# Gate and value weight blocks of a fused attention and two expert layers: prepared in two steps during the attention, with another order of the products behind it

## Chip, cores and metric

One core of one Trainium2 chip. The metric is the device time of one launch in microseconds (us). TensorE does the matrix products, VectorE and ScalarE the elementwise work, GpSimd a part of it, SyncE issues all DMA transfers. Most executions of this kernel agree within 0.3%.

## The reference, cut to what matters

```python
attn_out = _attn_ref(q, k, v)             # 2 batches, 8 heads, 576 positions, 64 wide
x = attn_out.transpose(0, 2, 1, 3).reshape(1152, 512)
# first layer: one wide gated layer, 1536 hidden
g = x @ w_gate
x = (g * (1 / (1 + np.exp(-g)))) * (x @ w_val) @ w_out
# second layer: 8 experts of 1024 hidden, weighted by a routing matrix P of x
for e in range(8):
    out += P[:, e:e+1] * (np.maximum(x @ w1[e], 0) @ w2[e])
```

The attention is the sum of a local one (positions closer than 4) and a pooled one (groups of 4 positions averaged). The weights w_gate, w_val and w_out come as 64-bit floats.

## The kernel before

Three parts follow each other: the attention, the first (gated) layer, the experts. Every product of the layers is made from 16-bit operands: a number is scaled by a power of two and split into a high and a low half, and three products (high x high, high x low, low x high) add up in PSUM (`mm3`, line 171; `split`, line 164).

**Attention** (`attention`, line 346). 16 heads, two to a pair, 8 pairs. For each head: scores on TensorE, row minima and sums on VectorE, exponentials on ScalarE, the division on GpSimd, a transpose on TensorE (`turn`), and for each pair the products with v (`combine`, line 432). `combine` ends with the split of the pair's result into `xhl`, the input of the first layer; the VectorE instruction of that split is kept in `x1_done` (line 463). The scores run 4 heads ahead (`AHEAD`). The generator yields once for each of the 4 heads ahead, then three times a head; in line 655 the loop over it counts these yields as n, so that the pair pr is combined at n = 9 + 6 pr. The SyncE queue loads q, k and v of the pairs (lines 297 to 314).

**Gate and value weights.** The hidden dimension of the first layer is cut into 12 blocks of 128 (`KF1`). A block holds the gate and the value weights for all 512 inputs, 1 MB as 64-bit floats. `prep_gv(f)` (line 207) does all of its preparation: the load into one of two `raw` buffers (line 185); the conversion `from_f64` (line 188) into one of two `cv` buffers, one step on ScalarE (Abs at line 200 or Relu at line 197) and four on VectorE (lines 201 or 198, then 202, 203, 204); the row maxima on ScalarE (line 215), which write over `raw`; the maximum over the partitions (`allmax`, line 147), by two small products and a reduction on VectorE for blocks below `NSHORT` = 6 and on GpSimd (line 155) for the others; the power of two (lines 138 to 141); and the split into one of five `wA` buffers (`WB`), on ScalarE (line 168) and VectorE (line 169). Blocks below `NX` = 3 use Abs, the others Relu.

**First layer.** The positions are cut into two chunks: chunk 0 has 512 columns, all of batch 0, and chunk 1 has 640, the rest. `gv_step(c, f)` (line 506) makes the 24 (chunk 0, 512 wide) or 48 (chunk 1, 320 wide) products of block f with chunk c, then the activation on ScalarE and the product with the value on VectorE (line 547). The first three steps of chunk 0 ("early") use tanh in place of silu and the PSUM banks of a pool that the attention leaves free. A `wA` buffer is free again when both chunks have used its block. `prep_wo(i)` (line 223) prepares two blocks of w_out out of the same `raw` and `cv` buffers. `act_split(c)` (line 556) scales and splits the twelve activations of a chunk; its scales need all of w_out's (line 559), and each of its tiles takes a slot that the activation before has left. `w_out(c)` (line 577) multiplies them by w_out, four output columns of 36 products for chunk 0.

**Order.** Before, blocks 0 and 1 are prepared in the attention's loop (`PREP_AT`), at n = 9 and 21, each behind the last `x1_done` (`tc.issue_after` puts an instruction behind the given one on the same engine, and does nothing on other engines). Then `moe1_step(f)` (line 661) prepares block f + 2, runs chunk 0 on block f and chunk 1 on block f - 3 (`LAG`), and prepares w_out blocks at every second step:

```python
        if f + np_ < KF1:
            prep_gv(f + np_, gv_done.get((0, f - 1)))
        if f < KF1:
            gv_step(0, f, f < NX)
        if f >= LAG:
            gv_step(1, f - LAG, False)
```

The final order on each engine is not this one: a planner walks the program, takes of the instructions that are ready by its own estimate of times the one that stands first in the program, and so may bring later work forward into gaps. On the chip each engine then keeps the planned order.

Of the kernel before, what the change touches and what calls it, by code (L numbers as in the profile page):

```python
# [8 lines left out]
F16 = mybir.dt.float16  # L9
BF16 = mybir.dt.bfloat16  # L10
U32 = mybir.dt.uint32
AF = mybir.ActivationFunctionType
# [7 lines left out]
NT, DM = 1152, 512  # L20
# [6 lines left out]
KF1 = F1 // P  # L27
# [9 lines left out]
FAR = 1.0e9  # L37
DW = 2 * SD
DO = NW * P
PREP_AT = (9, 21)  # L40
AHEAD = 4
NX = 3
LAG = 3
WB = 5
W2B = 6
HSC = 2.0 ** -20
# [3 lines left out]
NWARM = 5  # L50
NQ = 3
V4B = 4
NSHORT = 6
QDV = (0, 1, 2)
SPLITS = (2, 4, 2, 0)

# [2 lines left out]
def tile_kernel(ctx, tc, qT, kT, vw, vd4, wgv, wo, wg2, w1, w2, out):  # L59
# [15 lines left out]
    def tmp(n, nm):  # L75
        return wp.tile([P, 16], F32, tag="tmp", bufs=56, name=nm)[:, :n]
# [106 lines left out]
    def load_f64(src, nm):  # L183
        raw = wp.tile([P, 2 * DM, 2], U32, tag="raw", bufs=2, name=f"raw{nm}")
        nc.sync.dma_start(raw.rearrange("p n w -> p (n w)"), src.bitcast(U32))
        return raw

    def from_f64(raw, nm, relu):

        f = mp.tile([P, 2 * DM], F32, tag="cv", bufs=2, name=f"cv{nm}")
        o, lo, hi = f.bitcast(U32), raw[:, :, 0], raw[:, :, 1]
        h = hi.bitcast(F32)
        if relu:
            A.activation(f, h, AF.Relu, scale=-1.0)
            V.scalar_tensor_tensor(f, h, HI_MIN, f, op0=ALU.max, op1=ALU.max)  # L198
        else:
            A.activation(f, h, AF.Abs)  # L200
            V.tensor_scalar(f, f, HI_MIN, None, op0=ALU.max)
        V.tensor_scalar(o, o, 3, 0x3FFFFFF8, op0=ALU.logical_shift_left, op1=ALU.bitwise_and)  # L202
        V.scalar_tensor_tensor(o, hi, 0xC0000000, o, op0=ALU.bitwise_and, op1=ALU.bitwise_or)  # L203
        V.scalar_tensor_tensor(o, lo, 29, o, op0=ALU.logical_shift_right, op1=ALU.bitwise_or)  # L204
        return f

    def prep_gv(f, after=None):

        w = wp.tile([P, 7 * 4 * P], F16, tag="wA", bufs=WB, name=f"gv{f}")
        w = w[:, :4 * DM].rearrange("p (a n) -> p a n", a=2)  # L210
        raw = load_f64(wgv[f], f"g{f}")
        with tc.issue_after(after.ins) if after else nullcontext():
            src = from_f64(raw, f"g{f}", f >= NX)
            mx = tmp(1, f"mxg{f}")
            A.activation(raw.rearrange("p n w -> p (n w)").bitcast(F16)[:, :2 * DM], src, AF.Abs, accum_out=mx)  # L215
            s, gv_inv[f] = pow2(allmax(mx, 1, f"gv{f}", f < NSHORT), 1, f"gv{f}")
            split(w[:, 0], w[:, 1], src, s)
        gv_w[f] = w
# [4 lines left out]
    def prep_wo(i):  # L223

        ws = [m2.tile([P, 2, DM], F16, tag="wo", bufs=KF1, name=f"wo{i}{j}") for j in range(2)]
        src = from_f64(load_f64(wo[i], f"o{i}"), f"o{i}", False).rearrange("p (j n) -> p j n", j=2)
        mx = tmp(2, f"mxo{i}")
        for j in range(2):
            A.activation(ws[j][:, 0], src[:, j], AF.Abs, accum_out=mx[:, j:j + 1])
        s, _ = pow2(mx, 2, f"wo{i}", wo_inv[:, 2 * i:2 * i + 2])  # L230
        for j in range(2):
            split(ws[j][:, 0], ws[j][:, 1], src[:, j], s[:, j:j + 1])
            wo_w[2 * i + j] = ws[j]
# [83 lines left out]
    x1_done = []  # L317
# [186 lines left out]
    gv_done = {}  # L504
# [51 lines left out]
    def act_split(c):  # L556
        nh = CH[c][1]
        sc = cp.tile([P, KF1], F32, name=f"sc{c}")
        V.tensor_tensor(sc, amx[c], wo_inv, op=ALU.mult)
        s, ia[c] = pow2(allmax(sc, KF1, f"a{c}"), 1, f"a{c}")  # L560
        V.tensor_scalar(sc, wo_inv, s, None, op0=ALU.mult)
        for f in range(KF1):
            t = (m2 if c else mp).tile([P, 2, nh], F32, tag=f"act{c}", bufs=KF1 + 1, name=f"ahl{c}_{f}")
            t = t.rearrange("p u n -> p (u n)").bitcast(F16).rearrange("p (a n) -> p a n", a=2)
            ins = split(t[:, 0], t[:, 1], act[c, f], sc[:, f:f + 1])
            ahl[c, f] = t
        return ins
# [85 lines left out]
    load_v(1)  # L653
    first = tmp(1, "first")
    for n, _ in enumerate(attention()):
        if n in PREP_AT:
            prep_gv(PREP_AT.index(n), x1_done[-1])
    np_ = len(PREP_AT)
    G.partition_all_reduce(first, ones[:, :1], channels=P, reduce_op=RED.max)

    def moe1_step(f):
        if f + np_ < KF1:
            prep_gv(f + np_, gv_done.get((0, f - 1)))
        if f < KF1:
            gv_step(0, f, f < NX)
        if f >= LAG:
            gv_step(1, f - LAG, False)
        if f >= NX and f < KF1:
            prep_wo((f - NX) // 2) if (f - NX) % 2 == 0 else None
        if f == KF1 - 1:  # L670
            for i in range((KF1 - NX + 1) // 2, KF1 // 2):
                prep_wo(i)
            act_split(0)

    for f in range(NX):
        moe1_step(f)
    ctxA.close()
    ctxP = ExitStack()
    psr = ctx.enter_context(tc.tile_pool(name="psr", bufs=1, space=PSUM, reuse_waits="tile"))
    psm = ctxP.enter_context(tc.tile_pool(name="psm", bufs=2, space=PSUM, reuse_waits="tile"))  # L680
    m2 = ctxM.enter_context(tc.tile_pool(name="m2", bufs=1, side="right", reuse_waits="tile"))
    for f in range(NX, KF1 + LAG):
        moe1_step(f)
    ins = act_split(1)
    ctxX.close()
    xp = ctx.enter_context(tc.tile_pool(name="xp", bufs=1, reuse_waits="tile"))
# [156 lines left out]
```

## Time and profile before

| | us |
|---|---|
| three runs | 1053.83, 1054.74, 1056.79; median 1054.74 |
| the profiled execution | 1054.22, of which the span is 1052.4 |
| busy in the span | TensorE 1017.5 (97%), VectorE 752.0 (71%), ScalarE 458.0 (44%), GpSimd 91.5 (9%) |

In the rows below PE is TensorE, PEld its loads of weights, DVE VectorE, ACT ScalarE, POOL GpSimd and SP SyncE; L176 is line 176 of the kernel. Times count from the start of the span. A busy time is a sum over the stretch named, and "x" gives the number of instructions. Idle time of an engine that isn't the bottleneck costs nothing by itself, so the stages are read one by one. In rows of a timeline the bracket at the end is the time that the engine sat idle before, and what ended it. In the rows of busy time by stretch the five columns after the length are PE, PEld, DVE, ACT and POOL. PEclk is the granted clock of TensorE as a share of its full 2.4 GHz.

### The profile page before, as it was taken

The page shows a single profiled execution, that of the slowest core. Times are in us where ns is not written, and L with a number is a line of the kernel's source. Part 1 is how long each engine was busy: PE and PEld are TensorE (multiplying, and loading weights), DVE is VectorE, ACT ScalarE, POOL GpSimd, SP SyncE. Part 2 cuts the span into 40 slices and gives each one's busy share as a digit, 9 for nine tenths or more (in the row PEclk, how much of TensorE's full clock was granted, in tenths as well). Part 3 has the DMA queues.
Part 4 walks back from the last instruction along what each step waited for, and adds up shares of the span by engine and source line. Part 5 has one row for each costly group of instructions (what it writes and reads, how often), then busy time and mean ns, then how long its engine had stood idle before and what let it go on. Part 6 is the DMA issues. An engine that isn't in the chain of part 4 may idle for free.

```text
span 1052.4 us, 16461 instructions
## 1 busy us (share of the span) xinstructions
PE 1017.5 (97%) x6549; PEld 651.2 (62%) x6549; DVE 752.0 (71%) x1552; ACT 458.0 (44%) x957; POOL 91.5 (9%) x125
## 2 busy tenths in 40 slices
PE   6989698999999999999999999999999999999998
PEld 5888254556567866665756756666575675666644
DVE  5695668886691999888759749758874974974631
ACT  6988365666460646345215314414521541441200
POOL 6794000000000200000000000000000000000000
PEclk9999898999999999999999999999999999999999
DMA  9623123331020022112112100301211210020011
GB/s 237 152 79 107 53 108 112 129 128 73 1 81 1 2 80 82 41 40 80 41 40 80 42 23 18 121 1 41 80 41 41 78 44 19 22 81 1 1 40 50
DMA packets 22459, 65.54 MB, mean 62 GB/s; under 512 B 12080, under 2 KB 12336, under 8 KB 15984
## 3 DMA queue, kind: packets, MB, share of 16 engines
q1 hardware_dynamic: 22384, 64.51, 18.0%
q8 instruction: 51, 0.84, 0.3%
q14 instruction: 24, 0.20, 0.1%
HBM read 62.14 MB, written 2.36 MB: 61 GB/s over the span
## 4 chain that ended last, share of the span: by engine, by line
PE 83%; DVE 8%; DMA 4%; ACT 3%; issue 2%; SPq 0%; POOL 0%; ACTq 0%
PE y L176 35%; PE p L176 30%; PE gv L176 7%; PE wo L176 7%; DMA rawg<-in_wgv 2%; DVE cvg L203 1%; PE o L449 1%; DVE cvg L204 1%; PE lgps L575 1%; DMA rawo<-in_wo 1%; ACT rawg L215 1%; DVE cvg L198 1%; DVE cvg L202 1%; DVE xhl L169 1%; DMA qz<-in_qT 0%
## 5 line engine op out<-in xcount | busy, mean ns | idle before, releaser
L176 PE MATMUL y<-w,hhl 128*128 128x512 f16 (+1 forms) x1752 | 396.2, 376 | 0.0
L176 PE MATMUL p<-bop,w 128*128 128x320 f16 (+1 forms) x2688 | 354.4, 286 | 0.8 <-DVE u L715 0.5
L176 PEld LDWEIGHTS <-w 128*128 128x128 f16 x2688 | 263.0, 98 | 90.6 <-issue 1.3
L176 PEld LDWEIGHTS <-hhl 128*128 128x128 f16 x1752 | 171.4, 98 | 178.2
L176 PE MATMUL gv<-xhl,gv 128*128 128x320 f16 (+1 forms) x864 | 147.1, 332 | 7.4 <-ACT gv L168 4.0
L743 ACT ACTIVATE hhl<-h 128x640 f16<-128x640 f32 (+1 forms) x128 | 83.2, 676 | 159.7 <-DVE h L715 159.4
L176 PEld LDWEIGHTS <-gv 128*128 128x128 f16 x864 | 84.9, 99 | 67.0 <-issue 10.5
L168 ACT ACTIVATE w<-r,s_w 128x256 f16<-128x256 f32 (+1 forms) x96 | 71.1, 783 | 115.7 <-PE y L176 86.3
L774 DVE SCALAR_TENSOR_TENSOR acc<-y,pe,acc 128x512 f32<-128x512 f32 (+1 forms) x64 | 47.3, 739 | 101.3 <-PE y L176 100.5
L744 DVE SCALAR_TENSOR_TENSOR hhl<-h,hhl 128x640 f16<-128x640 f32 (+1 forms) x128 | 94.3, 753 | 15.5 <-ACT hhl L743 14.4
L715 DVE SCALAR_TENSOR_TENSOR h<-p,u 128x256 f32<-128x256 f32 (+1 forms) x192 | 84.8, 452 | 19.2 <-PE p L176 13.4
L169 DVE SCALAR_TENSOR_TENSOR w<-r,s_w,w 128x256 f16<-128x256 f32 (+1 forms) x96 | 78.1, 832 | 16.8 <-ACT w L168 16.7
L176 PE MATMUL wo<-ahl,wo 128*128 128x320 f16 (+1 forms) x432 | 71.5, 326 | 0.0
L168 ACT ACTIVATE w<-cmb,s_w 128x512 f16<-128x512 f32 x64 | 43.0, 710 | 40.7 <-DVE cmb L262 38.0
L715 DVE SCALAR_TENSOR_TENSOR u<-p,u 128x320 f32<-128x320 f32 (+1 forms) x128 | 57.2, 447 | 4.1 <-PE p L176 3.2
L176 PEld LDWEIGHTS <-wo 128*128 128x128 f16 x432 | 42.3, 99 | 27.0
L155 POOL PARTITION_ALL_REDUCE g_w<-gm_w x16 | 5.9, 370 | 568.6 <-DVE gm_w L151 562.7
L732 ACT ACTIVATE s<-p 128x256 f32<-128x256 f32 (+1 forms) x64 | 25.4, 397 | 56.7 <-PE p L176 56.7
L145 DVE TENSOR_REDUCE mxw<-r 128x1 f32<-128x1024 f32 x32 | 37.5, 1212 | 12.7 <-DMA r<-in_w 12.7
L169 DVE SCALAR_TENSOR_TENSOR w<-cmb,s_w,w 128x512 f16<-128x512 f32 x64 | 46.1, 740 | 0.0
L282 ACT ACTIVATE j<-r 128x1024 f16<-128x1024 f32 x32 | 33.4, 1046 | 25.1 <-DMA r<-in_w 25.0
L715 DVE SCALAR_TENSOR_TENSOR u<-p,s 128x256 f32<-128x256 f32 (+1 forms) x64 | 28.8, 450 | 5.2 <-PE p L176 4.3
(205 smaller groups left out, 933.5 us busy)
## 6 DMA issues: line engine op xcount, KB each, us to landing
r<-in_w SPq DMA_DIRECT2D x32, 1024.0 KB, 4.8
rawg<-in_wgv SPq DMA_DIRECT2D x12, 1024.0 KB, 6.5
rawo<-in_wo SPq DMA_DIRECT2D x6, 1024.0 KB, 4.8
vz<-in_vw SPq DMA_DIRECT2D x16, 160.0 KB, 3.2
k<-in_kT SPq DMA_DIRECT2D x8, 288.0 KB, 6.3
qz<-in_qT SPq DMA_DIRECT2D x16, 144.0 KB, 5.2
v<-in_vd SPq DMA_DIRECT2D x8, 288.0 KB
out<-acc SPq DMA_DIRECT2D x8, 256.0 KB, 2.0
```

The source lines that it names most:

```text
L145: V.tensor_reduce(o, i, axis=axis, op=ALU.max, apply_absolute_value=True)
L168: return (A.activation(hi, src, AF.Copy, scale=s), V.scalar_tensor_tensor(lo, src, s, hi, op0=ALU.mult, op1=ALU.subtract))
L169: V.scalar_tensor_tensor(lo, src, s, hi, op0=ALU.mult, op1=ALU.subtract))
L176: T.matmul(ps, lhsT=wf(i, k), rhs=xf(j, k), start=n == 0, stop=n == 3 * nk - 1)
L198: V.scalar_tensor_tensor(f, h, HI_MIN, f, op0=ALU.max, op1=ALU.max)
L202: V.tensor_scalar(o, o, 3, 0x3FFFFFF8, op0=ALU.logical_shift_left, op1=ALU.bitwise_and)
L282: A.activation(junk, t[:, 2 * j:2 * j + 2].rearrange("p a n -> p (a n)"), AF.Abs, accum_out=mx[:, 2 * i + j:2 * i + j + 1])
L715: V.scalar_tensor_tensor(o, ps, HSC, u, op0=ALU.mult, op1=ALU.add)
L732: A.activation(s1, p1, AF.Copy, scale=HSC)
L743: ra = A.activation(t[:, 0], h, AF.Relu)
L744: rv = V.scalar_tensor_tensor(t[:, 1], h, 0.0, t[:, 0], op0=ALU.max, op1=ALU.subtract)
L774: V.scalar_tensor_tensor(acc[t][:, ds], ps, p[:, t:t + 1], acc[t][:, ds], op0=ALU.mult, op1=ALU.add)
```

## The change

`prep_gv` is cut into `conv_gv(f)` (load, conversion, row maxima) and `prep_gv(f)` (maximum, power of two, split). In the attention's loop block 0 is converted at n = 4, without a gate. At n = 9 + 6 pr, after the pair pr is combined, block pr is split (pr from 0 to 4) and block pr + 1 converted (pr from 0 to 5), both behind that pair's `x1_done`. Blocks 0 to 6 use Abs (`NABS` = 7), and blocks 0 to 4 the short maximum (`NSHORT` = 5). Behind the attention the three early steps of chunk 0 and its step 3 come first. Then, for g from 0 to 11: chunk 1's products with block g, the split of block g + 5, the conversion of block g + 7 or, from g = 5 on, one pair of w_out blocks, and from g = 1 to 8 chunk 0's products with block g + 3. The last two pairs of w_out blocks and the split of chunk 0's activations follow at g = 8.

```diff
-PREP_AT = (9, 21)
+NABS = 7
-LAG = 3
-NSHORT = 6
+NSHORT = 5
...
+    gv_src = {}
+
+    def gate(after):
+        return tc.issue_after(after.ins) if after else nullcontext()
+
+    def conv_gv(f, after=None):
+
+        raw = load_f64(wgv[f], f"g{f}")
+        with gate(after):
+            src = from_f64(raw, f"g{f}", f >= NABS)
+            mx = tmp(1, f"mxg{f}")
+            A.activation(raw.rearrange("p n w -> p (n w)").bitcast(F16)[:, :2 * DM], src, AF.Abs, accum_out=mx)
+        gv_src[f] = src, mx
+
     def prep_gv(f, after=None):
 
         w = wp.tile([P, 7 * 4 * P], F16, tag="wA", bufs=WB, name=f"gv{f}")
         w = w[:, :4 * DM].rearrange("p (a n) -> p a n", a=2)
-        raw = load_f64(wgv[f], f"g{f}")
-        with tc.issue_after(after.ins) if after else nullcontext():
-            src = from_f64(raw, f"g{f}", f >= NX)
-            mx = tmp(1, f"mxg{f}")
-            A.activation(raw.rearrange("p n w -> p (n w)").bitcast(F16)[:, :2 * DM], src, AF.Abs, accum_out=mx)
+        src, mx = gv_src[f]
+        with gate(after):
             s, gv_inv[f] = pow2(allmax(mx, 1, f"gv{f}", f < NSHORT), 1, f"gv{f}")
             split(w[:, 0], w[:, 1], src, s)
         gv_w[f] = w
...
     for n, _ in enumerate(attention()):
-        if n in PREP_AT:
-            prep_gv(PREP_AT.index(n), x1_done[-1])
-    np_ = len(PREP_AT)
+        pr, r = divmod(n - AHEAD - 5, 6)
+        if n == AHEAD:
+            conv_gv(0)
+        if r == 0 and 0 <= pr < NABS - 1:
+            if pr < WB:
+                prep_gv(pr, x1_done[pr])
+            conv_gv(pr + 1, x1_done[pr])
     G.partition_all_reduce(first, ones[:, :1], channels=P, reduce_op=RED.max)
 
-    def moe1_step(f):
...
     for f in range(NX):
-        moe1_step(f)
+        gv_step(0, f, True)
...
-    for f in range(NX, KF1 + LAG):
-        moe1_step(f)
+    gv_step(0, NX, False)
+    for g in range(KF1):
+        gv_step(1, g, False)
+        if g + WB < KF1:
+            prep_gv(g + WB)
+        if g + NABS < KF1:
+            conv_gv(g + NABS)
+        elif g + NX < KF1:
+            prep_wo(g + NABS - KF1)
+        if 0 < g < KF1 - NX:
+            gv_step(0, g + NX, False)
+            if g + NX == KF1 - 1:
+                for i in range(g + NABS - KF1 + 1, KF1 // 2):
+                    prep_wo(i)
+                act_split(0)
     ins = act_split(1)
```

## Rows read from the trace of the kernel before

**Rows 1.** Busy time by stretch: stretch, length, each engine, PEclk, DMA share, GB/s.
```profile
20.00:41.00 21.00, 18.64 (x158) 17.03 (x156) 10.76 (x39) 18.58 (x77) 18.45 (x23) 0.92 0.77 207
41.00:80.00 39.00, 34.48 (x295) 32.27 (x295) 34.82 (x71) 33.04 (x144) 33.33 (x33) 1.00 0.33 92
80.00:96.00 16.00, 16.00 (x154) 14.64 (x153) 9.30 (x35) 15.25 (x54) 10.48 (x12) 1.00 0.40 113
96.00:107.00 11.00, 11.00 (x75) 7.76 (x73) 6.25 (x16) 5.85 (x14) 0.38 (x1) 1.00 0.21 86
107.00:214.20 107.20, 91.30 (x506) 49.86 (x506) 81.09 (x140) 57.15 (x95) 2.38 (x4) 0.94 0.27 99
214.20:266.30 52.10, 52.10 (x349) 34.08 (x349) 38.80 (x78) 34.70 (x65) 1.92 (x3) 1.00 0.28 102
```

**Rows 2.** Timeline of TensorE around the gate and value products: start, length, what.
```profile
105.06 1.03 PE L449 MATMUL o<-at,vz 128*128 128x120 f32 x8
105.92 1.24 PE L176 MATMUL gv<-xhl,gv 128*128 128x512 f16 x5
114.40 0.58 PE L159 MATMUL sm_gv<-ident,mxg 128*1 128x128 f32 x2 [7.23 <-ACT rawg L215]
...
171.47 4.02 PE L176 MATMUL gv<-xhl,gv 128*128 128x512 f16 x9 [4.00 <-ACT gv L168]
...
259.74 6.68 PE L176 MATMUL gv<-xhl,gv 128*128 128x320 f16 x48
266.26 12.90 PE L176 MATMUL wo<-ahl,wo 128*128 128x512 f16 x59
...
288.38 7.93 PE L176 MATMUL wo<-ahl,wo 128*128 128x512 f16 x36
```

**Rows 3.** Instructions on the converted blocks: ns min/median/max, first and last start.
```profile
L202 DVE TENSOR_SCALAR cvg<-cvg x12: 631/686/694, 42.8 to 209.3; 128x1024 uint32<-128x1024 uint32 x12
L203 DVE SCALAR_TENSOR_TENSOR cvg<-rawg,cvg x12: 1207/1218/1671, 44.7 to 211.0; 128x1024 uint32<-128x1024 uint32 x12
L204 DVE SCALAR_TENSOR_TENSOR cvg<-rawg,cvg x12: 1206/1218/2115, 45.9 to 214.1; 128x1024 uint32<-128x1024 uint32 x12
L215 ACT ACTIVATE rawg<-cvg x12: 1039/1056/1077, 49.7 to 215.8; 128x1024 f16<-128x1024 f32 x12
L168 ACT ACTIVATE gv<-cvg,s_gv x12: 1132/1148/1212, 57.9 to 223.5; 128x1024 f16<-128x1024 f32 x12
L169 DVE SCALAR_TENSOR_TENSOR gv<-cvg,s_gv,gv x12: 1264/1284/2508, 59.8 to 225.2; 128x1024 f16<-128x1024 f32 x12
...
L198 DVE SCALAR_TENSOR_TENSOR cvg<-rawg,cvg x9: 1215/1215/1226, 108.1 to 207.5; 128x1024 f32<-128x1024 f32 x9
L200 ACT ACTIVATE cvg<-rawg x3: 1132/1146/1208, 22.9 to 62.3; 128x1024 f32<-128x1024 f32 x3
L201 DVE TENSOR_SCALAR cvg<-cvg x3: 675/677/683, 41.5 to 67.3; 128x1024 f32<-128x1024 f32 x3
```

**Rows 4.** Timeline of VectorE, small steps of block 0's scale.
```profile
55.41 0.27 DVE L160 TENSOR_REDUCE gr_gv<-sm_gv 1x1 f32<-1x128 f32 x1
...
56.34 0.15 DVE L139 TENSOR_SCALAR u_gv<-u_gv 128x1 uint32<-128x1 uint32 x1
```

**Rows 5.** DMA issues of the page: transfer, count, KB each, median us to landing.
```profile
rawg<-in_wgv SPq DMA_DIRECT2D x12, 1024.0 KB, 6.5
```

**Rows 6.** Who waited for whom, 0 to 100 us: total us, times, longest.
```profile
ACT k L357 <- DMA k<-in_kT: 5.2, 5, 1.4
```

**Rows 7.** Timeline of VectorE from the last evaluation of chunk 0.
```profile
240.49 0.75 DVE L547 SCALAR_TENSOR_TENSOR act<-gv,iv,act 128x512 f32<-128x512 f32 x1
...
247.20 0.88 DVE L547 SCALAR_TENSOR_TENSOR act<-gv,iv,act 128x640 f32<-128x640 f32 x1
...
267.71 0.75 DVE L169 SCALAR_TENSOR_TENSOR ahl<-act,sc,ahl 128x512 f16<-128x512 f32 x1
```

**Rows 8.** GpSimd's additions of line 374: ns min/median/max, first and last start.
```profile
L374 POOL TENSOR_TENSOR vdz<-vt x16: 445/451/3392, 16.1 to 89.5; 72x128 f32<-72x128 f32 x16
```

More of the change, by code (lines that the diff above doesn't have):

```diff
@@ L655, in tile_kernel @@
     for n, _ in enumerate(attention()):
-        if n in PREP_AT:
-            prep_gv(PREP_AT.index(n), x1_done[-1])
-    np_ = len(PREP_AT)
-    G.partition_all_reduce(first, ones[:, :1], channels=P, reduce_op=RED.max)
-    def moe1_step(f):
[L662 to L673, printed above, removed]
+        pr, r = divmod(n - AHEAD - 5, 6)
[5 more added lines that the diff above has]
+            conv_gv(pr + 1, x1_done[pr])
+    G.partition_all_reduce(first, ones[:, :1], channels=P, reduce_op=RED.max)
     for f in range(NX):
-        moe1_step(f)
+        gv_step(0, f, True)
     ctxA.close()
```

## Prediction

> **What bounds the kernel now.** I read the page first, then the busy time of each engine by stage, then TensorE's instructions in order of time, then the durations of the operations that the change moves. From 214 us to the end of the stage at 266 TensorE is busy all the time [rows 1], and 97% of the whole span; the profiled execution took 1054.22 us for a span of 1052.4, 0.5 below the median of 1054.74. So the change can win only ahead of 214 us. There are two stages there. The **attention** (to 106 us) is crowded: between 41 and 80 us VectorE is busy 34.82 of 39 us, ScalarE 33.04, GpSimd 33.33 and TensorE 34.48; from 80 to 96 us TensorE is full and ScalarE has 0.75 us left [rows 1]. The **gate/value stage** from 107 to 214 us is where TensorE idles: 91.30 busy of 107.20 us, 15.9 us lost, at a mean granted clock of 0.94, so part of it ran at the lower level, 1.2 for 2.4 GHz [rows 1]. The reader is to see there that TensorE runs out of finished weight blocks: 7.23 us for the maximum of block 3, later 4.00 us for a split [rows 2].
>
> How much is there to win? The attention's last product starts at 105.06 us; at 107.16 the first gate block's 24 products for chunk 0 are done, and the first w_out product starts at 266.26 [rows 2]: 159.1 us. A 512-wide product costs (12.90 - 7.93)/(59 - 36) = 0.2161 us, two uninterrupted runs of w_out subtracted so that their tails cancel; a 320-wide one (266.26 - 259.74)/48 = 0.1358 [rows 2]. A chunk-0 step is thus 24 x 0.2161 = 5.19 us and a chunk-1 step 48 x 0.1358 = 6.52. Left to do are 11 x 5.19 + 12 x 6.52 = 135.3 us. **23.8 us is the most that can be won**: 15.9 of idle time, the rest products at the lower clock level, small maximum products and waits inside the order.
>
> **The change, part by part.** *More blocks in the attention.* Before, blocks 0 to 2 are converted and split by 107 us. After, 0 to 6 are to be converted and 0 to 4 split. One conversion costs VectorE 0.677 + 0.686 + 1.218 + 1.218 = 3.80 us and ScalarE 1.146 + 1.056 = 2.2; one split costs VectorE 1.284 and ScalarE 1.148 [rows 3], and its scale four VectorE steps of 0.15 and a reduce of 0.27 [rows 4], so VectorE 2.2 in all. By stage:
> - 20 to 41 us: conversion 0 moves here from 41 to 47 us. VectorE has 10.2 us free, GpSimd only 2.55 [rows 1]. The two-input steps (2.4 us) hold GpSimd up; bounds 0 and 2.4, I take 1.2, since half of its free time is there.
> - 41 to 80 us: three conversions as before, but three splits in place of one: 2 x 2.2 = 4.4 us more for VectorE, which has 4.2 free. An engine whose queue waits on three others won't reach 100%: at its present 89%, 4.4/0.89 = 4.9 us longer. Bounds 0.2 (every gap filled) and 4.9; I take 4.9, because GpSimd is as full as VectorE. ScalarE's 2.3 more fit in its 6 free.
> - 80 to 96 us: conversion 4 comes in, one split stays one: 3.8 for VectorE (6.7 free) and 2.2 for ScalarE (0.75 free): 1.5 us longer, bounds 0 and 2.2.
> - 96 us and later: split 4, conversions 5 and 6, some 9.8 us of VectorE beside 15 us or more of early products that need none of it: nothing. Were that cover gone, it costs up to 9.8.
>
> Together the attention's end moves back by **7.6 us** (bounds 0.2 and 9.5).
> *Gates.* The prepared steps stand behind a pair's last VectorE split, on the same engine: no semaphore, but the score minima of later heads queue behind them; that is in the 4.9.
> *Loads.* The same twelve, in the same SyncE queue, but loads 2 to 6 now go between the pairs' loads. 6.5 us from issue to landing, and ScalarE waits only 5.2 us in five waits for k now [rows 5, 6]. I take nothing; the bound is the last rival.
> *Abs in place of Relu* for blocks 3 to 6: VectorE 1.215 becomes 0.677 [rows 3], 2.2 us in all, already in the sums above. *The maximum of block 5* goes from TensorE to GpSimd, which does nothing then: nothing.
> *The new order of products.* Five ready blocks give 4 x 5.19 + 6.52 = 27 us of products before block 0's buffer must be refilled, and each round brings 11.71 us of products for one conversion, one split and two evaluations, about 8 us of VectorE (4.3 + 2.2, and 0.75 + 0.88 for the evaluations [rows 7]). So late weights (7.23 and 4.00) vanish. What stays is short waits for the evaluation that frees PSUM: 15.9 - 11.2 = 4.7 us before. I take **4** (bounds 0, as from 214 to 266 us with VectorE 74% busy, and 8).
> *The end of the stage.* Before, four chunk-1 steps follow the last chunk-0 step; after, three. The chain behind it is: the last chunk-0 evaluation ends at 241.24, the twelfth activation split at 268.46 [rows 7], while w_out's twelfth block is first used 33 products in, at 266.26 + 33 x 0.2161 = 273.4. 4.9 us of slack less one step of 6.52 makes 1.6 us of waiting. The last two w_out blocks are also prepared later against that step, and the scales need them: bounds 0 and 10 (two blocks' chains). I take **2.5**, near the row.
>
> Sum: 23.8 - 7.6 - 4 - 2.5 = 9.7 us won; 1054.22 - 9.7 = 1044.5 on the profiled execution, **1045 us** against the median. After the first w_out product all is TensorE-bound and moves rigidly.
>
> **A row against the change.** Where VectorE's two-input steps meet GpSimd's, one of the two is stretched: a split took 2.508 us where the median is 1.284, L204 2.115 for 1.218 [rows 3], and a GpSimd add 3.392 for 0.451 [rows 8]. The Trainium skill (SBUF — State Buffer, section "SBUF: two separate sides") calls the shared port pair an exclusive lock, held for a whole instruction, with the other side fully blocked. The rows agree that somebody waits; by the rule the whole added work would come on top of GpSimd's, which is the second rival below.
>
> **Rivals.** *The gaps hold it* (0.16): attention 3 us longer, short waits 2, none at w_out; 18.8 won, 1036. For: 10.2 and 6.7 us free on VectorE on either side of the crowd. Against: the middle has 4.2.
> *VectorE and GpSimd take turns throughout* (0.12): by 92 us two more conversions and two more splits' long steps, 2 x 3.80 + 2 x 1.284 = 10.2 us, lengthen GpSimd's run, plus ScalarE's 1.5: 23.8 - 11.7 - 6.5 = 5.6 won, 1049. For: the stretched rows. Against: GpSimd is idle 5.5 of 16 us from 80 us on [rows 1].
> *The change doesn't do what it says* (0.08): the order on each engine is planned from estimated times, and the gates only set an earliest point; blocks 3 and 4 may be split only after the attention. Then the 11.2 us of waits stay and the attention grows by 3: 23.8 - 11.2 - 4 - 2.5 - 3 = 3.1 won, 1051.6.
> *w_out waits its full 10 us* (0.06): 2.1 won, 1052.6.
> *Slower* (0.15): the queue of SyncE issues in order, so a 1 MB block load can stand in front of a pair's k and q. ScalarE takes k in its own order and stops there, with the exponentials behind it. Four pairs (4 to 7) at 6.5 us [rows 5] are 26 us; 23.8 - 26 - 6.5 = 8.7 lost, 1063. It decides from the point where the attention's last product starts later than 105 + 17 = 122 us. For: k is already waited for. Against: the DMA engines are less than half busy after 41 us [rows 1].
>
> **How the numbers follow.** The forecast itself has 0.43 (1039 to 1050). About 0.3% (3.2 us) is what a measurement here can tell from no change. Faster by more: 0.41 of the forecast, 0.16, 0.12 and 0.03 of the third rival make 0.72. Within: 0.02, 0.05, 0.06 make 0.13. Slower: 0.15. The range from 1034 to 1056 leaves out the slow rival and a corner of the fast one, 0.18.
>
> **What would show it.** Right: block 4's split ends before or within 5 us of the attention's last product, which starts near 113 us; after it TensorE has no idle time above 2 us until w_out, whose first product starts near 256 to 257 us; a short wait inside w_out's first column, ended by the activation split. Wrong: block loads in front of k in SyncE's queue with ScalarE waiting on DMA; attention past 122 us; waits for weight splits above 4 us; or a first w_out pass with gaps of 5 us and more.

## The result, and the profile after

The changed kernel takes 1045.34 us (median of 4 runs, 1044.92 to 1047.23), the kernel before, beside it, 1054.28: a ratio of 0.9915 (0.9893 to 0.9936), 8.9 us faster. The profiled execution took 1045.74 us, its span is 1043.7, 8.7 below that of before.

Busy time by stretch of the kernel after, with the columns of [rows 1]:

```profile
20.00:41.00 21.00, 16.69 (x152) 14.52 (x151) 13.39 (x40) 17.99 (x74) 15.69 (x19) 1.00 0.95 260
41.00:80.00 39.00, 32.25 (x283) 29.76 (x281) 34.54 (x73) 32.87 (x131) 32.40 (x32) 0.96 0.44 122
80.00:96.00 16.00, 15.67 (x115) 14.46 (x116) 13.35 (x42) 13.96 (x51) 9.91 (x11) 0.89 0.29 90
113.00:204.00 91.00, 91.00 (x557) 54.48 (x556) 59.45 (x107) 48.54 (x84) 3.02 (x7) 1.00 0.26 93
204.00:257.00 53.00, 51.33 (x326) 31.64 (x324) 44.64 (x86) 34.03 (x66) 0.70 (x2) 1.00 0.27 100
257.00:311.00 54.00, 51.22 (x294) 29.80 (x294) 41.37 (x74) 30.44 (x48) 1.17 (x2) 0.94 0.10 39
```

From 113 to 204 us TensorE is busy for all of 91.00 us, where the kernel before lost 15.9 of 107.20 [rows 1]. The attention has become less dense in exchange: TensorE does 32.25 us of work from 41 to 80 where it did 34.48, at a granted clock of 0.96, and of 0.89 from 80 to 96, where it had 1.00 in both. A second loss lies behind 204, where before there was none.

The timeline of TensorE after, which answers to [rows 2]:

```profile
113.34 1.70 PE L459 MATMUL o<-at,vz 128*128 128x120 f32 x14
114.88 134.78 PE L175 MATMUL gv<-xhl,gv 128*128 128x512 f16 x836
249.50 5.95 PE L175 MATMUL wo<-ahl,wo 128*128 128x512 f16 x26
259.10 12.16 PE L175 MATMUL wo<-ahl,wo 128*128 128x512 f16 x42 [3.65 <-DVE ahl L168]
271.59 1.02 PE L175 MATMUL wo<-ahl,wo 128*128 128x512 f16 x4 [0.33 <-DVE ahl L168]
...
334.04 4.09 PE L175 MATMUL p<-bop,w 128*128 128x256 f16 x36
```

The waits of 7.23 and 4.00 us are gone, and no bracket is left from 114.88 to 249.50. The attention's last product starts 8.3 us later, w_out 16.8 us earlier, the first expert product (342.77 before) 8.7 us earlier; behind that one the two run alike (1052.4 - 342.77 = 709.6, 1043.7 - 334.04 = 709.7). So all that was won and lost lies ahead of it, in three places:

- **Attention**: 28 gate products are done by 114.88, where 24 were by 107.16 [rows 2]. 7.72 less 4 x 0.2161 is **6.9 us** later for the same work.
- **Gate stage**: 134.62 us (114.88 to 249.50) for the 836 products, 260 of 0.2161 and 576 of 0.1358 us, which are 134.4: **0.2 us** lost.
- **w_out to the first expert product**: 84.5 us, before 76.5: **8.0 us** lost. 3.65 us of it are the long stop, some 0.7 us the short ones, and some 3 us that the 42 products behind the stop took 12.16 us, where 42 x 0.2161 is 9.1: the granted clock over the stretch from 257 us is 0.94 of 2.4 GHz, so a part ran at the lower level.

23.8 - 6.9 - 0.2 - 8.0 = 8.7. VectorE shows what is late at w_out's start (timeline of the kernel after; `u_wo` and `sc` are the power of two of the last w_out pair and the activations' scale, `cmb` and `mxw` belong to the experts' w1, `ahl` with 128x512 is a split of chunk 0, with 128x640 of chunk 1):

```profile
240.72 0.17 DVE L137 TENSOR_SCALAR u_wo<-mxo 128x2 f32<-128x2 f32 x1 [1.40 <-ACT wo L239]
...
241.40 0.17 DVE L569 TENSOR_TENSOR sc<-amx,wo_inv 128x12 f32<-128x12 f32 x1
...
244.39 0.68 DVE L271 TENSOR_TENSOR cmb<-r,r 128x512 f32<-128x512 f32 x1
...
246.32 0.23 DVE L571 TENSOR_SCALAR sc<-wo_inv,s_a 128x12 f32<-128x12 f32 x1
...
247.87 0.75 DVE L168 SCALAR_TENSOR_TENSOR ahl<-act,sc,ahl 128x512 f16<-128x512 f32 x1 [0.74 <-ACT ahl L167]
...
253.67 2.33 DVE L144 TENSOR_REDUCE mxw<-r 128x1 f32<-128x1024 f32 x2
...
256.05 2.34 DVE L144 TENSOR_REDUCE mxw<-r 128x1 f32<-128x1024 f32 x2
258.31 1.54 DVE L168 SCALAR_TENSOR_TENSOR ahl<-act,sc,ahl 128x512 f16<-128x512 f32 x2
```

Two things are to be seen. The scale stands behind the last w_out pair, whose power of two comes 10.5 us after chunk 0's last evaluation (230.21); before, the first scale step came 3.9 us behind it (244.40 against 240.49). And w1's steps stand among the scale's and the splits': 4.67 us of maxima between the fourth split and the fifth. TensorE's stop ends when the split of 258.31 is there. Before, the combine steps (`cmb`) stood among the scale's too, from 243.80 us on; the maxima came at 269.97, behind the last split of [rows 7].

### The profile page after: what moved, and what is told of

Read it like the earlier page. It is cut to its first block, busy times and chain, and to the rows that moved or that the text cites. A ratio compares the mean times of both kernels' runs of the same rounds, so it can differ in the third digit from the quotient of the medians.

```text
span 1043.7 us, 16467 instructions
## 1 busy us (share of the span) xinstructions
PE 1015.4 (97%) x6545; PEld 650.8 (62%) x6545; DVE 750.0 (72%) x1551; ACT 457.1 (44%) x957; POOL 92.8 (9%) x126
## 4 chain that ended last, share of the span: by engine, by line
PE 87%; DVE 6%; DMA 3%; ACT 2%; issue 2%; SPq 0%; POOL 0%; ACTq 0%; DVEq 0%
PE y L175 36%; PE p L175 30%; PE gv L175 12%; PE wo L175 5%; DMA rawg<-in_wgv 1%; DVE ahl L168 1%; PE o L459 1%; DMA k<-in_kT 1%; PE lgps L585 1%; ACT ahl L167 1%; DMA qz<-in_qT 1%; PE s L394 0%; DVE mxw L144 0%; PE o L451 0%; DVE stm L403 0%
## 5 line engine op out<-in xcount | busy, mean ns | idle before, releaser
L175 PE MATMUL gv<-xhl,gv 128*128 128x320 f16 (+1 forms) x864 | 141.1, 326 | 0.1
L168 DVE SCALAR_TENSOR_TENSOR w<-r,s_w,w 128x256 f16<-128x256 f32 (+1 forms) x96 | 78.1, 832 | 16.8 <-ACT w L167 16.7
L175 PE MATMUL wo<-ahl,wo 128*128 128x320 f16 (+1 forms) x432 | 74.9, 333 | 4.0 <-DVE ahl L168 4.0
```

What stands on the lines that cost most here:

```text
L168: V.scalar_tensor_tensor(lo, src, s, hi, op0=ALU.mult, op1=ALU.subtract))
L175: T.matmul(ps, lhsT=wf(i, k), rhs=xf(j, k), start=n == 0, stop=n == 3 * nk - 1)
```

## The experiments

All were timed beside the kernel before, whose median was 1054.28 us beside the changed kernel, 1054.39 for 1 to 4, 1054.42 for 5 to 8, 1055.74 for 9 to 11 and 1055.43 for 12; across these sets the ratios compare more safely than the times. The three times are starts in the profiled execution: the attention's last product, the first of w_out, the first of the experts.

| kernel | last attention | w_out | experts | w_out to experts | ratio (interval) |
|---|---|---|---|---|---|
| before | 105.06 | 266.26 | 342.77 | 76.5 | 1 |
| after | 113.34 | 249.50 | 334.04 | 84.5 | 0.9915 (0.9893 to 0.9936) |
| 1 chunk 0 leads | 112.97 | 252.02 | 339.07 | 87.1 | 0.9960 (0.9945 to 0.9975) |
| 2 scales without w_out | 114.97 | 251.12 | 335.27 | 84.2 | 0.9918 (0.9900 to 0.9935) |
| 3 w1 behind the splits | 109.85 | 246.01 | 324.37 | 78.4 | 0.9851 (0.9834 to 0.9869) |
| 4 block 0 converted later | 112.64 | 252.03 | 336.58 | 84.6 | 0.9919 (0.9901 to 0.9937) |
| 5 chunk 1 closer behind | 111.16 | 248.46 | 327.67 | 79.2 | 0.9875 (0.9854 to 0.9896) |
| 6 after, no pooled sums | 111.30 | 247.46 | 332.01 | 84.6 | 0.9910 (0.9887 to 0.9933) |
| 7 before, no pooled sums | 104.34 | 264.85 | 341.37 | 76.5 | 0.9986 (0.9974 to 0.9998) |
| 8 old preparation | 104.02 | 248.83 | 333.39 | 84.6 | 0.9920 (0.9900 to 0.9940) |
| 9 = 3 and 5 | 112.19 | 249.49 | 328.39 | 78.9 | 0.9895 (0.9877 to 0.9914) |
| 10 = 3, 5 and 8 | 104.03 | 245.87 | 327.79 | 81.9 | 0.9859 (0.9841 to 0.9877) |
| 11 before, with 3 | 104.09 | 263.90 | 341.59 | 77.7 | 1.0008 (0.9991 to 1.0026) |
| 12 = 3 and 8 | 101.17 | 246.00 | 324.34 | 78.3 | 0.9862 (0.9846 to 0.9879) |

The theories on w_out's start were three: the cover (three chunk-1 steps behind the last chunk-0 step, where four stood), the late w_out blocks, and w1's steps in VectorE's queue.

**1. The old order of the products, with the new preparation.**

```diff
         gv_step(1, g, False)
...
-        if 0 < g < KF1 - NX:
-            gv_step(0, g + NX, False)
-            if g + NX == KF1 - 1:
-                for i in range(g + NABS - KF1 + 1, KF1 // 2):
-                    prep_wo(i)
-                act_split(0)
+        if g < KF1 - NX - 1:
+            gv_step(0, g + NX + 1, False)
+        if g + NX == KF1 - 1:
+            for i in range(g + NABS - KF1 + 1, KF1 // 2):
+                prep_wo(i)
+            act_split(0)
```

> The changed kernel with the old order of products: chunk 0's step g + 4 follows chunk 1's step g, so four chunk-1 steps stand behind the last chunk-0 step in place of three. Theory 1 (cover: w_out waits because one chunk-1 step of 6.52 us less lies over the chain of activation splits): the waits at w_out's start (3.65, 0.33 and 0.35 us, and the slow clock behind them, 8 us in all) shrink to under 2, and the kernel takes 1037 to 1040 us. Theory 2 (late w_out blocks: the scales of chunk 0's splits need the last pair of w_out blocks, ready only at 241.2 us, 10 us behind the last chunk-0 evaluation): the last pair is no earlier, w_out starts and waits as in the changed kernel, 1044 to 1048 us. If the order of products is what keeps TensorE fed in the gate stage, new waits for weight splits show there, a few us in all.

1051.00 us, 5.7 above the changed kernel, with the longer cover; it lies outside both expected ranges. Timelines of VectorE (first two lines) and of TensorE:

```profile
244.76 0.17 DVE L137 TENSOR_SCALAR u_wo<-mxo 128x2 f32<-128x2 f32 x1 [0.60 <-ACT wo L239]
...
252.51 0.75 DVE L168 SCALAR_TENSOR_TENSOR ahl<-act,sc,ahl 128x512 f16<-128x512 f32 x1
```

```profile
114.50 134.91 PE L175 MATMUL gv<-xhl,gv 128*128 128x512 f16 x836
252.02 1.01 PE L175 MATMUL wo<-ahl,wo 128*128 128x512 f16 x2 [2.60 <-ACT ahl L167]
...
260.57 3.00 PE L175 MATMUL wo<-ahl,wo 128*128 128x512 f16 x12 [3.47 <-DVE ahl L168]
```

The cover falls as the cause. Each chunk-1 step now ends one chunk-0 step (5.19 us) later, and with it come free the buffers of the later blocks: the last pair's power of two is 4.0 us later than after. In the gate stage there is no wait for weights here either: the 836 products take 134.91 us, 0.5 over their sum of 134.4. So what the new order adds, it adds through w_out's blocks.

**2. Scales of chunk 0 without w_out's powers of two** (which changes that part of the computation).

```diff
-        V.tensor_tensor(sc, amx[c], wo_inv, op=ALU.mult)
+        wi = wo_inv if c else ones[:, :KF1]
+        V.tensor_tensor(sc, amx[c], wi, op=ALU.mult)
         s, ia[c] = pow2(allmax(sc, KF1, f"a{c}"), 1, f"a{c}")
-        V.tensor_scalar(sc, wo_inv, s, None, op0=ALU.mult)
+        V.tensor_scalar(sc, wi, s, None, op0=ALU.mult)
```

> The changed kernel, whose scales of chunk 0's activation splits leave out w_out's powers of two (so the output is another, and the splits no longer wait for the last w_out pair; the same instructions otherwise). Theory 1 (cover): the splits start some 3 us behind the last chunk-0 evaluation, but the wait at w_out's start stays within 2 us of the changed kernel's 4.3 us of idle time; 1043 to 1046 us. Theory 2 (late w_out blocks): chunk 0's first activation split starts near 236 us in place of 247, the wait at w_out's start is gone, 1036 to 1039 us.

1045.86 us, no gain. It doesn't settle the theory: the first scale step moved to 234.10, but the planned order kept the next one, the maximum over the blocks, at 242.89 behind the last w_out pair, and the first split at 248.74. The data wait was taken away and the place in the queue stayed.

**3. w1's preparation behind the last activation split on both engines.** The gates are the two instructions of chunk 1's last split (`ins = act_split(1)`), one on ScalarE, one on VectorE; only the first was there. The expectations of 9, 11 and 12 call it the last split of w_out's first operand; it is this one, behind the splits of both chunks.

```diff
-    with tc.issue_after(ins[0].ins):
+    with tc.issue_after(ins[0].ins), tc.issue_after(ins[1].ins):
         prep_w1(0)
```

> The changed kernel with the preparation of the first expert's weights held behind the last activation split on VectorE too (before: on ScalarE alone), so its four maxima (4.6 us of VectorE between 253.7 and 258.4 us) no longer stand among chunk 0's splits. Theory 3 (the planned order of VectorE puts other work into the chain): the 3.65 us wait at w_out's start goes and with it most of the slow clock, 4 to 6 us won, 1039 to 1042 us. Theories 1 and 2: the chain starts too late whatever stands in it, at most 1 us won, 1044 to 1046 us; a later wait for w1 at the first expert would cost on top.

1038.84 us, 6.5 below the changed kernel, the fastest of all. VectorE, then TensorE:

```profile
237.92 0.17 DVE L569 TENSOR_TENSOR sc<-amx,wo_inv 128x12 f32<-128x12 f32 x1
...
241.09 0.23 DVE L571 TENSOR_SCALAR sc<-wo_inv,s_a 128x12 f32<-128x12 f32 x1
242.50 0.75 DVE L168 SCALAR_TENSOR_TENSOR ahl<-act,sc,ahl 128x512 f16<-128x512 f32 x1 [1.18 <-ACT ahl L167]
...
250.56 2.36 DVE L168 SCALAR_TENSOR_TENSOR ahl<-act,sc,ahl 128x512 f16<-128x512 f32 x3
```

```profile
246.01 13.76 PE L175 MATMUL wo<-ahl,wo 128*128 128x512 f16 x62
260.10 1.46 PE L175 MATMUL wo<-ahl,wo 128*128 128x512 f16 x6 [0.33 <-DVE ahl L168]
```

Between the two scale steps lie 3.17 us, after 4.92; the splits run through without the maxima, which now start at 272.45 us, the long stop is gone, and from 257 to 311 us the granted clock is 1.00. 6.1 us of the loss of 8.0 come back. (In the profiled execution the attention also ended 3.5 us sooner, with the same instructions in the same order up to 244 us; the 6.5 us are of the medians.)

**4. Block 0 converted behind pair 0, not ahead of it.**

```diff
-        if n == AHEAD:
-            conv_gv(0)
         if r == 0 and 0 <= pr < NABS - 1:
+            if pr == 0:
+                conv_gv(0, x1_done[0])
```

> The changed kernel with block 0's conversion put behind pair 0's split, where it was before, in place of the early point. My step (VectorE's and GpSimd's free time from 20 to 41 us takes it nearly for nothing, and 41 to 80 us is full): pair 0's split comes back from 45.2 to 43 to 44 us, but the conversion lengthens the full stretch by 3 to 4 us; the attention's last product 2 to 4 us later, 1047 to 1049 us. Rival (the early stage lost most of the time: pair 0 came 4.3 us later than before): pair 0's split is back at 41 us, the attention ends 2 to 4 us earlier, 1041 to 1043 us.

1045.48 us, as the changed kernel; both guesses missed. The split of pair 0 came at 42.98 us, that of pair 1 at 59.28. Timelines of VectorE, before and then after:

```profile
40.87 0.74 DVE L169 SCALAR_TENSOR_TENSOR xhl<-x,s_x,xhl 128x512 f16<-128x512 f32 x1
51.47 2.20 DVE L169 SCALAR_TENSOR_TENSOR xhl<-x,s_x,xhl 128x512 f16<-128x512 f32 x1
...
75.48 1.73 DVE L169 SCALAR_TENSOR_TENSOR xhl<-x,s_x,xhl 128x512 f16<-128x512 f32 x1
```

```profile
45.17 0.96 DVE L168 SCALAR_TENSOR_TENSOR xhl<-x,s_x,xhl 128x512 f16<-128x512 f32 x1
...
47.69 2.05 DVE L202 SCALAR_TENSOR_TENSOR cvg<-rawg,cvg 128x1024 uint32<-128x1024 uint32 x1
...
49.81 2.54 DVE L203 SCALAR_TENSOR_TENSOR cvg<-rawg,cvg 128x1024 uint32<-128x1024 uint32 x1
...
58.72 0.73 DVE L168 SCALAR_TENSOR_TENSOR xhl<-x,s_x,xhl 128x512 f16<-128x512 f32 x1
...
83.85 0.73 DVE L168 SCALAR_TENSOR_TENSOR xhl<-x,s_x,xhl 128x512 f16<-128x512 f32 x1
```

4.3 us late at pair 0, 7.3 at pair 1, 8.4 at pair 3: most of the stretch lies ahead of 60 us. One execution tells this only roughly: experiment 3, with the same instructions, has the first two at 44.77 and 55.46. But over all the profiles pair 1's split starts between 55.46 and 60.53 us with the new preparation, between 49.49 and 52.59 with the old one. Where the first conversion stands in the attention doesn't show in the time.

**5. Chunk 1 two blocks behind chunk 0 instead of three.** One step less of cover, but every block's buffers come free sooner.

```diff
-    gv_step(0, NX, False)
     for g in range(KF1):
...
-        elif g + NX < KF1:
+        elif g + NX <= KF1:
             prep_wo(g + NABS - KF1)
-        if 0 < g < KF1 - NX:
-            gv_step(0, g + NX, False)
-            if g + NX == KF1 - 1:
+        if 0 < g < KF1 - 2:
+            gv_step(0, g + 2, False)
+            if g == KF1 - NX:
```

> The changed kernel with chunk 1 a further step ahead: chunk 0's step g + 2 follows chunk 1's step g, so only two chunk-1 steps (13 us) stand behind the last chunk-0 step, and every wA buffer, and with it the last w_out pair, comes free one chunk-0 step (5.2 us) earlier. Theory 1 (cover): one more step of cover is lost, w_out waits 5 to 7 us longer, 1050 to 1053 us. Theory 2 (late w_out blocks, held up through the wA and cv buffers): the chain of chunk 0's activation splits starts 4 to 5 us earlier against w_out, of the 8 us lost there 4 to 6 come back, 1039 to 1042 us. The first chunk, whose order in the attention is the same, ends its attention as before this edit.

1040.78 us, 4.6 below the changed kernel (their intervals just touch). Timeline of TensorE:

```profile
248.46 12.61 PE L175 MATMUL wo<-ahl,wo 128*128 128x512 f16 x56
261.77 1.46 PE L175 MATMUL wo<-ahl,wo 128*128 128x512 f16 x6 [0.71 <-DVE ahl L168]
```

The last w_out power of two comes at 233.99, the first split at 242.03; w1's maxima still stand among the splits, at 252.63, but the splits are 5.8 us ahead and the stop is 0.71 us. So the late blocks are a cause as well: the stop needs late scales and the maxima together, and either cure is enough.

**6, 7. GpSimd's sums of the pooled v left out** of the changed kernel and of the one before (the pooled values are then zero, so that part is not computed).

```diff
-        G.memset(vdz[i][:, :, 0, 64:], 0.0)
-        G.memset(vdz[i][:, :, 1, :64], 0.0)
+        G.memset(vdz[i], 0.0)
...
-            vt = ap.tile([HS, 2, 2, P], F32, tag="vt", bufs=1, name=f"vt{pr}")
-            G.tensor_tensor(vt[:, 0], v4[:, :, 0], v4[:, :, 1], op=ALU.add)
-            G.tensor_tensor(vt[:, 1], v4[:, :, 2], v4[:, :, 3], op=ALU.add)
-            for j in range(2):
-                h = slice(64 * j, 64 * j + 64)
-                G.tensor_tensor(vd[:, :, j, h], vt[:, 0, :, h], vt[:, 1, :, h], op=ALU.add)
```

> The changed kernel without GpSimd's sums of the pooled values (left out: lines 380 to 384, so the pooled part of the output is zero), some 19 us of GpSimd's work in the attention. To be read beside the same edit of the kernel before. Turn-taking (VectorE's and GpSimd's steps stretch each other, which made the attention some 7 us longer): with a quarter of GpSimd's work gone most of that goes, and the gain over the kernel before grows from 9 to 13 to 15 us. Occupancy (VectorE itself is full from 41 to 80 us): the gain stays at 8 to 10 us, though both kernels may be a little faster.

> The kernel before, with the same part left out. Turn-taking: it gains less than the changed kernel does, 0 to 3 us. Occupancy: both gain the same within 1 us.

1044.08 and 1052.92 us: 1.3 below the changed kernel and 1.5 below the kernel before; the difference is 8.8, with the sums 8.9. The intervals leave some 2 us open, but not 13 to 15. So the longer attention is not made by these 32 additions meeting VectorE's steps; the rest of GpSimd's work stayed in.

**8. The old preparation with the new order.** In the program blocks 0 and 1 are prepared whole in the attention, 2 to 6 behind it, without the gates of before, and with the changed kernel's Abs; the planner brings the conversions of 2 and 3 forward into it.

```diff
-        pr, r = divmod(n - AHEAD - 5, 6)
-        if n == AHEAD:
-            conv_gv(0)
-        if r == 0 and 0 <= pr < NABS - 1:
-            if pr < WB:
-                prep_gv(pr, x1_done[pr])
-            conv_gv(pr + 1, x1_done[pr])
+        if n in (9, 21):
+            f = (9, 21).index(n)
+            conv_gv(f, x1_done[-1])
+            prep_gv(f, x1_done[-1])
...
     for f in range(NX):
+        conv_gv(f + 2)
+        prep_gv(f + 2)
         gv_step(0, f, True)
+    conv_gv(5)
+    conv_gv(6)
```

> The changed kernel's order of products, with two blocks prepared whole in the attention, at the points of the kernel before, and blocks 2 to 6 converted behind the attention. My sum: the attention's last product is back near 105 to 106 us, but the waits for weights behind it return (11 us in all, the first of 5 to 8 us), 1048 to 1051 us. Rival (the order alone feeds TensorE): no wait above 2 us behind the attention, 1038 to 1042 us. Rival (the preparation alone does it): as the kernel before, 1053 to 1056 us.

1045.68 us, as the changed kernel, in none of its three expected ranges. The attention is back to its old length, and the waits for weights that the five ready blocks were to remove don't return; the longest behind the attention is this one (timeline of TensorE):

```profile
118.15 4.49 PE L175 MATMUL gv<-xhl,gv 128*128 128x512 f16 x20 [1.79 <-DVE gv L168]
```

What stood in the way of block 3, for whose maximum TensorE waited 7.23 us before, is to be seen in VectorE's timelines, of the kernel before and then of this experiment:

```profile
107.44 0.74 DVE L536 SCALAR_TENSOR_TENSOR act<-gv,iv,act 128x512 f32<-128x512 f32 x1
108.10 1.22 DVE L198 SCALAR_TENSOR_TENSOR cvg<-rawg,cvg 128x1024 f32<-128x1024 f32 x1
```

```profile
92.49 0.74 DVE L200 TENSOR_SCALAR cvg<-cvg 128x1024 f32<-128x1024 f32 x1
```

Before, ScalarE had done the block's first step at 90.74 us (L197, from 89.59), but `prep_gv(3)` was gated behind the evaluation of block 0 (107.44), so VectorE took the block up only at 108.10, though it was busy for no more than 6.25 of the 11 us from 96 to 107 [rows 1]. Here, without the gate, it took the same block up at 92.49. The kernel before without its gates was not run.

**9 to 11. The cures together, with either preparation; and the w1 gate on the kernel before.** The edits are those of 3 and 5; of 3, 5 and 8; and of 3.

> The edits of the two faster runs together: second chunk two gate blocks behind the first, and the preparation of w1 behind the last split of w_out's first operand on VectorE too. Apart they took 6.5 us (w1 behind the splits) and 4.6 us (two blocks behind) off the changed kernel. If they cure two halves of the loss at w_out's start (one the w1 maxima among the splits, the other the late w_out blocks), together they can't take more than the 8.0 us that were lost there plus what the order gives: 1035 to 1038.5, first product of w_out before 247 us, no stop in it over 0.4 us. Rival: both cure the same loss (the stop of 3.65 us and the low clock behind it), and the one adds nothing to the other: 1038.5 to 1041.

> The same two edits, with the old preparation of the gate blocks (two whole blocks inside the attention, the others behind it). If the two-step preparation inside the attention is worth nothing net in the new order, as its single run said, this is the same as the run above within 2 us. If its price (an attention some 7 us longer) is paid back only through w_out's start, which these edits now cure by themselves, this is 3 to 6 us faster than the run above: 1030 to 1035. If its blocks are needed once the second chunk follows closer, there are waits for weights again between 104 and 180 us, and this is 3 to 6 us slower: 1040 to 1044.

> The kernel before with w1's preparation held behind the last split of w_out's first operand on VectorE too. In the kernel before the w1 maxima (269.97 us) already stand behind that split (267.71 us). Theory: the hold is worth something only where the change brought those maxima in among the splits, so here there is no change: 1053 to 1055.5. Rival: it is a gain of its own, apart from the change: 1048 to 1051.

1043.71, 1040.24 and 1056.46 us, with a kernel before of 1055.74. The cures don't add up: 9 loses about as much at w_out as 5 does (78.9 and 79.2 us), and as a whole it is slower than 3 alone, by the ratios too. The first of its expectations, 1035 to 1038.5, is wrong; it misses its rival's range too, by 2.7, of which 1.3 are the slower kernel before. Part of the gap to 3 is the attention's scatter, 2.3 of 4.0 us in the profiles; what remains is not settled. 10 is 3.5 us faster than 9, as its second expectation had the difference but not the time (1030 to 1035), with the shorter attention and no wait above 0.4 us between it and w_out, though it takes 81.9 us from w_out to the experts: its last w_out power of two comes at 241.63, where 9 has it at 235.04: with chunk 1 this close, blocks prepared in the attention do bring w_out's forward. 11 shows no change, 1.0 us above its expected range beside a kernel before that was slower too: the hold moved w1's maxima from 269.97 us to 289.81, and there was nothing to cure.

**12. The w1 gate and the old preparation** (edits of 3 and 8).

> The new order with the old preparation (two whole blocks in the attention, the rest behind it), and w1's preparation held behind the last split of w_out's first operand on VectorE too; the second chunk stays three blocks behind. Theory: the two-step preparation is paid for by the attention's length and brings nothing net, w_out's loss of 8 us is that of the w1 maxima and of the clock behind the long stop, and is cured here as it was with the new preparation: attention's last product at 104 to 105 us, w_out's first at 244 to 249, 78 to 80 us from there to the first expert product, 1037.5 to 1041. Rival: the two blocks more that are ready at the attention's end are what brings the late w_out blocks forward; without them the scales come late, 82 us or more at w_out as in the last run with the old preparation, 1041 to 1045.

1039.83 us, within the theory's range, 0.9862 against 0.9851 for experiment 3, with overlapping intervals. Timeline of TensorE:

```profile
101.17 1.25 PE L459 MATMUL o<-at,vz 128*128 128x120 f32 x10
...
106.27 2.75 PE L175 MATMUL gv<-xhl,gv 128*128 128x512 f16 x12 [0.32 <-DVE act L546]
...
109.58 2.75 PE L175 MATMUL gv<-xhl,gv 128*128 128x512 f16 x12 [0.25 <-DVE u_gv L137]
112.48 1.04 PE L175 MATMUL gv<-xhl,gv 128*128 128x512 f16 x4 [0.16 <-ACT gv L167]
115.32 4.49 PE L175 MATMUL gv<-xhl,gv 128*128 128x512 f16 x20 [1.80 <-DVE gv L168]
...
123.37 122.79 PE L175 MATMUL gv<-xhl,gv 128*128 128x512 f16 x780 [0.25 <-DVE u_gv L137]
246.00 13.75 PE L175 MATMUL wo<-ahl,wo 128*128 128x512 f16 x62
```

The attention's last product is 8.7 us sooner than in experiment 3 (109.85), w_out's first comes at the same time, 246.00 and 246.01. The 8.7 us are given back behind the attention: 16 gate products fewer are done by its end (12 against 28, 3.5 us), the brackets add up to 2.8, and the small products for the maxima, now on TensorE's path, with the remaining gaps make the rest. With three blocks between the chunks, five ready blocks are worth what they cost, and no more.

## Why the prediction was right, and where it wasn't

**The total** was right: 1045 forecast, 1045.34 measured, faster. Two terms of the sum were off, by 3.8 us and by 5.5, in opposite directions; that they nearly cancel is luck.

**The attention, 7.6 us; measured 6.9.** The size was near, in part by luck: experiment 3, with the same instructions in the attention, ends it 3.5 us sooner. That it is longer is beyond the scatter: its last product starts between 101.17 and 105.06 us in the six profiles with the old preparation, between 109.85 and 114.97 in the eight with the new. Its distribution wasn't right: the step took 1.2 us from 20 to 41 and 4.9 from 41 to 80; 4.3 had gone by pair 0 and 7.3 by pair 1. The free time of VectorE from 20 to 41 us covered nothing: there it has 7.6 us left and the pair is late all the same. Experiments 8 and 12 show that the preparation moved in makes the attention longer, 4 that one conversion's place doesn't decide it. The steps that failed are the 1.2 us put on 20 to 41 us and the weighing of ScalarE by its free time alone. What that left out can be read at one place: ahead of 52.39 us ScalarE stood 2.6 us for a conversion's last VectorE step, with the exponentials of later heads behind it in its queue, and TensorE then stood 2.69 us for a VectorE step behind the same conversion (shown in the last section). How the rest divides among VectorE's time, ScalarE's and the loads that now keep the DMA engines 95% busy from 20 to 41 us (77% before) was not told apart.

**Short waits in the gate stage, 4 us; measured 0.2,** at the lower bound, 0. The step failed that read the kernel before's 4.7 us as waits for evaluations and carried them over. Two of these waits (timeline of TensorE before):

```profile
129.13 0.38 PE L159 MATMUL sm_gv<-ident,mxg 128*1 128x128 f32 x2 [1.22 <-ACT rawg L215]
...
145.14 2.75 PE L176 MATMUL gv<-xhl,gv 128*128 128x512 f16 x12 [0.52 <-DVE act L547]
```

Only 2.6 us of them end at an evaluation (0.52, 0.52, 0.62 and 0.92); 2.1 us (1.22, 0.25, 0.25 and 0.36) are for weights like the long ones. All of them are gone with the old order of products as well (0.5 us lost in experiment 1), so the new order isn't needed for that; what took them away was not isolated.

**w_out's start, 2.5 us; measured 8.0,** inside its bounds of 0 and 10. The failed step is "4.9 us of slack less one step of 6.52 makes 1.6 us of waiting". It took the cover as what counts, and VectorE's queue as it stood before. Experiment 1 lengthened the cover and lost 5.7 us, 5 shortened it and won 4.6. The bound's mechanism, the late last two w_out blocks, was the right one, and it needed a second that the prediction didn't have: w1's maxima, which the planner brought in among the splits (holding them and the combine steps back was worth 6.5 us in experiment 3). It also left out the lower clock behind the stop, some 3 us.

**"So late weights (7.23 and 4.00) vanish"** was right as a fact, and for the wrong reason. In experiment 8 only two blocks are split by the attention's end (block 2 at 109.43 us) and the longest wait behind it is 1.79 us. The five ready blocks aren't needed to remove the 7.23 us. The traces point to the gate, behind which block 3's conversion stood for 17 us (experiment 8). The gates are left out, and Abs is in, in the changed kernel and in experiments 1 and 8 alike, so what the order or the preparation would do without that was not taken apart.

So the gain belongs to the parts otherwise than argued: with chunk 0 leading, the new preparation, together with Abs and without the gates, is worth 0.4% of the time, some 4 us (experiment 1); the order with chunk 1 leading adds 0.45%, near 5 us; and with that order the preparation adds nothing that these runs can tell (8 against after, 12 against 3).

**The rivals.** *The gaps hold it*: no, the attention paid. *Turns with GpSimd*: steps are stretched indeed, L203 took 2.54 us at 49.81 for 1.22, but the gain with and without 32 of GpSimd's additions is 8.9 and 8.8. The stretched rows agree with the exclusive lock of the Trainium skill (SBUF — State Buffer, "SBUF: two separate sides"); the price for the whole kernel, 1049, didn't hold. *Doesn't do what it says*: no, block 4's split ran at 107.64, before the attention's last product. *w_out waits its full 10 us*: 8.0, but the other terms made room. *Slower*: ScalarE's wait for k was 4.7 us in four waits, before 5.2 in five [rows 6], and the last product started at 113.34, not past 122.

Of the marks set out to look for, these came: the last product near 113 us, no idle time above 2 us until w_out, a wait early in w_out ended by a split (in its first two columns, which the plan now interleaves, six products to a block). w_out's first product came at 249.50, not at 256 to 257. That mark didn't follow from the sum, whose 2.5 us were to be lost inside w_out: 266.26 less 23.8 - 7.6 - 4 is 254.1. The 4.6 us from there to 249.50 are the short waits that didn't come and the 0.7 us of the attention.

## What to carry to other kernels

When a stage stops waiting, the stage behind it starts sooner, and its first wait should be worked out from the new queue: list what the planner may now bring in ahead of the chain, and hold work of the next stage back on every engine that it uses, not on one. Here that one line was worth 6.5 us, on the kernel before nothing. When a change has several parts, time each alone: here, with the old gates left out, either the order or the early preparation leaves no wait above 2 us until w_out, and with the new order the preparation adds nothing that these runs can tell. And ask of a wait first whether the program itself holds the awaited step back: block 3's stood ready for 17 us behind a gate.

## What was not expected of the hardware

A stop of 3.65 us cost TensorE nearly as much again: the 42 products behind it took 0.29 us each where 0.2161 is usual, the granted clock over the stretch being 0.94; without the stop (experiment 3) it was 1.00. Behind a stop of the same length the products of experiment 8 lost 2.1 us (30 in 8.61 us) and those of experiment 6 1.8 (24 in 6.94).

And the attention's length differs between executions of the same instructions: experiment 3 has the changed kernel's, in the same order on every engine up to 244 us, and its last product of the attention started at 109.85 us against 113.34. That difference reached w_out's start unshortened (246.01 against 249.50). The traces show where it began (VectorE in experiment 3, then TensorE in the changed kernel):

```profile
47.15 1.23 DVE L202 SCALAR_TENSOR_TENSOR cvg<-rawg,cvg 128x1024 uint32<-128x1024 uint32 x1
...
48.44 2.02 DVE L203 SCALAR_TENSOR_TENSOR cvg<-rawg,cvg 128x1024 uint32<-128x1024 uint32 x1
```

```profile
53.58 0.59 PE L391 MATMUL s<-maskb,identb 128*128 128x512 bf16 x1 [2.69 <-DVE x L468]
```

In the changed kernel these two VectorE steps took 2.05 and 2.54 us (experiment 4), while GpSimd was at work all the time from 47.20 to 52.84. TensorE's wait behind them was 2.69 us there and 1.19 in experiment 3, and the clock granted from 41 to 80 us was 0.96 against 1.00 in experiment 3, from 80 to 96 us 0.89 against 1.00. Not all of the scatter is of this kind: experiments 8 and 12, the same instructions up to w_out as well, lie 2.9 us apart at the attention's last product (104.02 and 101.17) with the same granted clocks, 0.92 from 20 to 41 us and 1.00 from there to 107.
